# A third PSUM bank for the score gradients of two attention sweeps, taken from the sums and from a recurrent chain

## The chip, the cores and the metric

The kernel runs on one core of a Trainium2 chip. The metric is the device time of one execution in microseconds (us), the median of several. Runs of one kernel lie within 0.4% of each other; chips differ by about as much. So kernels are compared by ratios: a ratio is the mean time of a kernel's fast runs over the mean of the fast runs of the kernel before in the same rounds on the same chip, and thus not quite the ratio of the medians.

## The reference

Forward and backward of a gated mix of two attentions over 2048 tokens of width 576, in bf16. A has 32 query heads of size 18 and one shared key and value. B works on segments of 32 tokens, with eight memory rows that are the output of the segment before: 64 segments, one after the other.

```python
# A: shared-key attention (32 heads of 18)
scores = jnp.einsum('bhqd,bkd->bhqk', q, k) * Dh ** (-0.5)
p = _softmax(scores, axis=-1)
o = jnp.einsum('bhqk,bkd->bhqd', p, v)
# B: recurrent memory
for s in range(n_seg):
    h = jnp.concatenate([mem, xs], axis=1)
    ...
    o = jnp.einsum('bhte,hed->btd', o, Wo)
    mem = o[:, :M, :].copy()
# whole: g * a + (1 - g) * b, and the gradients of all weights, A_x and mem0
```

## The kernel before

A's attention is two sweeps of 1024 steps. A step makes scores S (128 x 1024), their exponential E on ScalarE, the gradient dP of the probabilities (two matmuls of 512 columns, one bank each of PSUM, where the kernel's matmuls leave their results), their products with E on VectorE, and adds E and the products into a sum (acc) on TensorE. B's recurrent chain is cut into 16 pieces a segment, and one piece is woven in front of each sweep step. Everything is issued in program order, and in the lines shown below TensorE starts its matmuls in that order. Shortened from the kernel:

```python
def weave(self, chain, sweep, per_piece):
    for _ in chain:                       # one piece of B's chain
        for _ in range(per_piece):        # per_piece = 1
            next(sweep, None)             # one step of A's sweep
# one step n of the backward sweep
mm_S(n + 1)                                               # b_S: one tile of 2 banks
dP = [psum.tile([P, 512], F32, name="b_dP", bufs=2) for _ in range(2)]
mm_u([t[:] for t in dP], n, 64)
ex(n + 1)                                                 # ScalarE: b_E = exp(b_S), 1024 columns
for i in range(2):                                        # VectorE: b_dS
    nc.vector.tensor_tensor(out=D_[n][:, i, :], in0=dP[i][:], in1=E_[n][:, i, :], op=ALU.mult)
# b_acc += products and E of step n - 1: 2 + 2 matmuls, column tiles of 32 (4 + 4 forward)
```

The 8 banks of 2 KiB are all in use. Forward: a_S 2, a_dP 2, a_acc 2, the chain's c_pj 1 and c_x 1. Backward: b_S 2, b_dP 2, b_acc 1, the chain's r_pj 2 and r_x 1. The chain needs two r_pj banks because it sums the new memory gradient in two column halves at once. Its backward pieces were: projection 3 and 2 of 5 row blocks, twice; dO transposed; score gradients; and then, with a `yield` (the end of a piece) after each,

```python
mem_grad(2, "r_pj", ...)   # 16 small matmuls
heads(2, 0)                # 32 matmuls of 288 columns into column half 0
mem_grad(0, "r_x", ...)
heads(2, 1)                # the same into column half 1
mem_grad(1, "r_x", ...)
heads(0, 0); heads(0, 1); heads(1, 0)      # a piece each
heads(1, 1); sums((0, 1))                  # one piece
sums((2, 3, 4))
```

## Time and profile before

| what | before |
|---|---|
| median of 3 runs | 6484.8 us (6476.7 to 6485.2) |
| forward sweep, first to last a_dP | 1928 us, 30.0 a segment of 16 steps |
| backward sweep, first to last b_dP | 1787 us, 27.3 a segment |
| all other stages together | 2756 us |
| TensorE, VectorE, ScalarE busy | 92%, 58%, 54% |

The two sweeps are 57% of the time, and only they are touched. A segment is read from the timeline as the distance between every sixteenth b_S (or a_S) matmul, a step as the distance between one and the next. The prediction below shows the lines.

### The profile page before, as it was taken

Reading aid. Unit: us, or ns where it says so; the run is one execution under the profiler, and the core shown is the slowest. Engines: PE = TensorE matmul, PEld = TensorE weight load, DVE = VectorE, ACT = ScalarE, POOL = GpSimd, SP = SyncE. Lnnn points to the kernel's source line nnn. Section 1 sums busy time; section 2 is a strip of 40 time slices with the busy share of each in tenths; the row PEclk is TensorE's granted clock in tenths of the full one; section 3 lists DMA queues with packets and bytes.
Section 4 is the critical chain, followed back from the end, with each engine's and each line's share of the span. In section 5 each row is a group of like instructions: output and inputs, shape, how many; then the busy total and the mean of one; then the engine's idle time right before and its main releaser. Section 6 shows DMA issues by size and latency. Waiting matters only on the chain. (4 is left out here: it accounts for less than half of the span.)

```text
span 6471.1 us, 208564 instructions
## 1 busy us (share of the span) xinstructions
PE 5931.5 (92%) x88611; PEld 3332.0 (51%) x88822; DVE 3769.7 (58%) x7061; ACT 3481.2 (54%) x5105; POOL 1952.8 (30%) x3451
## 2 busy tenths in 40 slices
PE   7898999999999995999879999999999899899997
PEld 5443444444444443778634444444444677675443
DVE  5336777777777773666568888888887211111111
ACT  3326777777777773656556767667776322211100
POOL 3002333333333333444423333333333111112212
PEclk9998999999999997999989999999999899999998
DMA  4636666666664435999854443333434799896643
GB/s 152 225 145 114 115 120 119 120 117 118 120 118 104 98 79 167 252 253 263 251 184 101 103 102 102 97 100 102 102 102 100 201 247 245 232 275 213 216 146 111
DMA packets 1368108, 991.94 MB, mean 153 GB/s; under 512 B 931613, under 2 KB 1184806, under 8 KB 1356486
## 3 DMA queue, kind: packets, MB, share of 16 engines
q1 hardware_dynamic: 1285030, 780.53, 49.3%
q0 software_dynamic: 82144, 198.05, 9.6%
q8 instruction: 696, 11.40, 0.7%
q14 instruction: 238, 1.95, 0.1%
HBM read 552.41 MB, written 384.76 MB: 145 GB/s over the span
## 5 line engine op out<-in xcount | busy, mean ns | idle before, releaser
L1424 DVE TENSOR_TENSOR a_W<-a_dP,a_E 128x512 bf16<-128x512 f32 x2048 | 1314.8, 684 | 478.9 <-PE a_dP L66 377.0
L1553 DVE TENSOR_TENSOR b_dS<-b_dP,b_E 128x512 bf16<-128x512 f32 x2048 | 1315.8, 684 | 328.0 <-PE b_dP L66 245.4
L1532 ACT ACTIVATE b_E<-b_S 128x1024 bf16<-128x1024 f32 x1024 | 1048.9, 1024 | 529.2 <-PE b_dP L66 393.6
L1394 ACT ACTIVATE a_E<-a_S 128x1024 bf16<-128x1024 f32 x1024 | 1052.1, 1027 | 134.5 <-PE a_dP L66 120.9
L66 PE MATMUL b_dP<-b_KV,b_QD 32*128 32x512 bf16 x2048 | 584.9, 382 | 5.2 <-DVE b_dS L1553 5.2
L66 PE MATMUL b_S<-b_KV,b_QD 32*128 32x512 bf16 x2048 | 401.6, 385 | 128.9 <-ACT b_E L1532 82.4
L66 PE MATMUL a_dP<-a_QD,l_KV 32*128 32x512 bf16 x2048 | 513.3, 382 | 1.0 <-DVE a_W L1424 0.8
L66 PE MATMUL w_acc<-w_d,w_h 128*128 128x512 bf16 (+1 forms) x2352 | 470.9, 379 | 2.5
L66 PE MATMUL a_S<-a_QD,l_KV 32*128 32x512 bf16 x2048 | 399.6, 383 | 74.3 <-ACT a_E L1394 72.4
L66 PE MATMUL r_pj<-WT,r_dT 128*32 128x288 bf16 x12288 | 447.0, 288 | 0.0
L66 PE MATMUL a_acc<-a_W,l_WK 128*32 128x512 bf16 x4096 | 410.5, 390 | 0.1
L66 PE MATMUL b_acc<-b_dS,b_SD 128*32 128x512 bf16 x2048 | 406.0, 393 | 0.0
L66 PE MATMUL b_acc<-b_E,b_SD 128*32 128x512 bf16 x2048 | 405.8, 393 | 0.0
L66 PE MATMUL a_acc<-a_E,l_VK 128*32 128x512 bf16 x4096 | 399.9, 380 | 0.0
L66 PEld LDWEIGHTS <-r_dT 128*32 128x32 bf16 x12288 | 330.6, 97 | 78.9 <-issue 1.1
L1027 DVE COPY y_T<-y_pt 128x512 bf16<-128x512 bf16 x256 | 96.8, 419 | 461.1 <-PE y_pt L71 443.6
L66 PEld LDWEIGHTS <-w_h 128*128 128x128 bf16 (+1 forms) x2400 | 213.1, 100 | 244.5 <-issue 3.4
L66 PEld LDWEIGHTS <-hm 128*32 128x32 bf16 x7680 | 207.0, 97 | 229.2 <-issue 15.0
L66 PEld LDWEIGHTS <-b_SD 128*32 128x32 bf16 x4096 | 105.3, 93 | 421.3 <-issue 420.3
L66 PEld LDWEIGHTS <-b_QD 32*128 32x128 bf16 x4096 | 142.9, 91 | 327.2 <-issue 245.3
L66 PEld LDWEIGHTS <-l_WK 128*32 128x32 bf16 x4096 | 105.3, 93 | 349.0 <-issue 348.9
L1013 ACT CAST y_tdk<-y_pk 128x512 bf16<-128x512 f32 x128 | 75.1, 587 | 379.9 <-PE y_pk L66 240.8
(410 smaller groups left out, 11558.8 us busy)
## 6 DMA issues: line engine op xcount, KB each, us to landing
b_QD<-qd_dram SPq DMA_DIRECT2D x256, 128.0 KB
b_SD<-sd_dram SPq DMA_DIRECT2D x256, 128.0 KB
dOx_dram<-p_tok SPq DMA_DIRECT2D x16, 1024.0 KB
c_vx<-vx_dram SPq DMA_DIRECT2D x256, 64.0 KB
krow_dram<-c_k POOLq DMA_DIRECT2D x64, 256.0 KB, 2.6
qrow_dram<-c_q POOLq DMA_DIRECT2D x64, 256.0 KB, 2.8
vrow_dram<-c_v POOLq DMA_DIRECT2D x64, 256.0 KB, 4.5
x_q<-qx_dram SPq DMA_DIRECT2D x32, 512.0 KB
```

Source lines behind the costliest of these rows:

```text
L66: return self.nc.tensor.matmul(out, lhsT, rhs, start=start, stop=stop, tile_position=tp, skip_group_check=True)
L1013: nc.scalar.copy(d[w][:, r, :], pk[:])
L1027: nc.vector.tensor_copy(T_[t][w][:], pt[:])
L1394: nc.scalar.activation(E_[n][:], S.pop(n)[:], ACT.Exp, scale=SCALEA)
L1424: nc.vector.tensor_tensor(out=W_[n][:, i, :], in0=dP[i][:], in1=E_[n][:, i, :], op=ALU.mult)
L1532: nc.scalar.activation(E_[n][:], S.pop(n)[:], ACT.Exp, scale=SCALEA)
L1553: nc.vector.tensor_tensor(out=D_[n][:, i, :], in0=dP[i][:], in1=E_[n][:, i, :], op=ALU.mult)
```

## The change

The intent: with three dP banks, the second dP matmul of a step no longer has to wait for the last product of the step before. Forward, the bank comes from the sums: one a_acc bank, so a new sum may start only when ScalarE has copied out the old one, and its first four matmuls are put off to the start of the next step. Backward, the bank comes from the chain: it finishes one column half before it begins the other, so one r_pj bank is enough, and its 48 head units (4 matmuls each) are dealt out anew.

```diff
 # backward chain
-            for j in range(2):
-                pj = psum.tile([P, 512], F32, name="r_pj", bufs=2)
-                for kts in ((0, 1, 2), (3, 4)):
+            pj = [psum.tile([P, 512], F32, name=nm, bufs=1) for nm in ("r_pj", "r_x")]
+            for k, parts in enumerate((((0, (0, 1, 2, 3)),), ((0, (4,)), (1, (0, 1))), ((1, (2, 3, 4)),))):
 ...
+            units = iter([(wi, hf, u) for hf in range(2) for wi in (2, 0, 1) for u in range(8)])
+            def heads(n):                       # n units of 4 matmuls
 ...
-            mem_grad(2, "r_pj", ...)
+            mem_grad(2, "r_x", ...)
 # pieces now: mem_grad 2 | mem_grad 0, 4 units | 4 units, mem_grad 1 | 6 | 6, x transposed | 4
 #             | 6 | 6, sums 0-1 | 6 | 6 | sums 2-4
 # forward sweep
+                if n > 1 and n % 16 == 1:
+                    acc = psum.tile([P, 512], F32, name="a_acc", bufs=1)
+                    acc_mm(acc, n - 1, E_, self.VK, True, False)
                 if n + 1 < NP_:
                     mm_S(n + 1)
-                dP = [psum.tile([P, 512], F32, name="a_dP", bufs=2) for _ in range(2)]
+                dP = [psum.tile([P, 512], F32, name="a_dP", bufs=3) for _ in range(2)]
 ...
-                if n % 16 == 0:
-                    acc = psum.tile([P, 512], F32, name="a_acc", bufs=2)
-                acc_mm(acc, n, E_, self.VK, n % 16 == 0, False)
+                if n == 0:
+                    acc = psum.tile([P, 512], F32, name="a_acc", bufs=1)
+                if n % 16 or n == 0:
+                    acc_mm(acc, n, E_, self.VK, n == 0, False)
 # backward sweep
-                dP = [psum.tile([P, 512], F32, name="b_dP", bufs=2) for _ in range(2)]
+                dP = [psum.tile([P, 512], F32, name="b_dP", bufs=3) for _ in range(2)]
```

More of the change, by code (lines that the diff above doesn't have):

```diff
@@ L846, in b_chain_bwd @@
             dOm = sp.tile([P, 8, E], BF16, name="r_dOm", bufs=1)
-            for j in range(2):
-                pj = psum.tile([P, 512], F32, name="r_pj", bufs=2)
-                for kts in ((0, 1, 2), (3, 4)):
-                    self.proj_part(pj, d_, self.WoT, j, kts)
-                    if s == NSEG - 1 and j == 0 and kts[0] == 3:
-                        self.load_WT()
-                    if kts[0] == 3:
-                        self.evac(dOm[:, 4 * j:4 * j + 4, :].rearrange("p u e -> p (u e)"), pj[:], use="s")
-                    yield
+            pj = [psum.tile([P, 512], F32, name=nm, bufs=1) for nm in ("r_pj", "r_x")]
+            for k, parts in enumerate((((0, (0, 1, 2, 3)),), ((0, (4,)), (1, (0, 1))), ((1, (2, 3, 4)),))):
+                for j, kts in parts:
+                    self.proj_part(pj[j], d_, self.WoT, j, kts)
+                    if kts[-1] == 4:
+                        self.evac(dOm[:, 4 * j:4 * j + 4, :].rearrange("p u e -> p (u e)"), pj[j][:], use="s")
+                if s == NSEG - 1 and k == 1:
+                    self.load_WT()
+                yield
             src = self.mem_T(dOm, psum, "r_x", 1)
@@ L886, in b_chain_bwd @@
             ph = {}
-            def heads(wi, hf):
-                if hf not in ph:
-                    ph[hf] = psum.tile([P, 288], F32, name="r_pj", bufs=2)
-                for u in range(8):
+            units = iter([(wi, hf, u) for hf in range(2) for wi in (2, 0, 1) for u in range(8)])
+            def heads(n):
+                for _ in range(n):
+                    wi, hf, u = next(units)
+                    if hf not in ph:
+                        ph[hf] = psum.tile([P, 288], F32, name="r_pj", bufs=1)
                     for g in range(4):
@@ L895, in heads @@
                                 start=(wi == 2 and u == 0), stop=(wi == 1 and u == 7), tp=(0, 32 * g))
-                if wi == 1:
-                    nc.scalar.copy(hs[:, 288 * hf:288 * hf + 288], ph[hf][:])
+                    if wi == 1 and u == 7:
+                        nc.scalar.copy(hs[:, 288 * hf:288 * hf + 288], ph[hf][:])
             def sums(kts):
@@ L904, in mem_grad @@
             def mem_grad(wi, name, pairs):
-                pg = psum.tile([P, 8, 32], F32, name=name, bufs=2 if name == "r_pj" else 1)
+                pg = psum.tile([P, 8, 32], F32, name=name, bufs=1)
                 for u in range(8):
@@ L912, in b_chain_bwd @@
             blk = lambda t, u0=0: [f(t[:, u0 + u]) for u in range(8)]
-            mem_grad(2, "r_pj", ((rows(mrow["dx"], E), [seln] * 8), (rows(dOm), blk(PqB))))
+            mem_grad(2, "r_x", ((rows(mrow["dx"], E), [seln] * 8), (rows(dOm), blk(PqB))))
             dSq = to_q((dS[:, 1, :],), "ds", nc.vector)
-            yield
-            heads(2, 0)
             yield
@@ L920, in b_chain_bwd @@
             self.expand(dSqB[:], dSq[:, 0, :, 0:8], 8)
+            heads(4)
             yield
-            heads(2, 1)
-            yield
+            heads(4)
             mem_grad(1, "r_x", ((rows(mrow["dx"]), [seln] * 8), (rows(mrow["q"]), blk(dSqB))))
@@ L928, in b_chain_bwd @@
             yield
-            heads(0, 0)
+            heads(6)
+            yield
+            heads(6)
             xq = to_q((pT[:, 0, :], dS[:, 0, :]), "x", nc.gpsimd)
@@ L934, in b_chain_bwd @@
             yield
-            heads(0, 1)
+            heads(4)
             yield
-            heads(1, 0)
+            heads(6)
             yield
-            heads(1, 1)
+            heads(6)
             pm = psum.tile([P, NKT, 8], F32, name="r_x", bufs=1)
             sums((0, 1))
+            yield
+            heads(6)
             if s:
                 PqB = p_blocks(nxt["pT"])
+            yield
+            heads(6)
             yield
```

## The prediction

> **What bounds the kernel now.** First the page: shares, then the costliest rows.
>
> ```profile
> PE 5931.5 (92%) x88611; PEld 3332.0 (51%) x88822; DVE 3769.7 (58%) x7061; ACT 3481.2 (54%) x5105; POOL 1952.8 (30%) x3451
> ...
> L1553 DVE TENSOR_TENSOR b_dS<-b_dP,b_E 128x512 bf16<-128x512 f32 x2048 | 1315.8, 684 | 328.0 <-PE b_dP L66 245.4
> L1532 ACT ACTIVATE b_E<-b_S 128x1024 bf16<-128x1024 f32 x1024 | 1048.9, 1024 | 529.2 <-PE b_dP L66 393.6
> ```
>
> No engine but TensorE is near full, and its 92% is modelled time. The change touches two sweeps: forward (a_dP matmuls, 508.5 to 2436.8 us by the view of that tile) and backward (b_dP, 3252.3 to 5039.6 us). Each is 1024 steps woven one to one with pieces of a recurrent chain, 16 to a segment. So I took the timeline of a segment and measured each step from its score matmul (b_S) to the next. A step with a light piece:
>
> ```profile
> 4019.85 0.39 PE L66 MATMUL b_S<-b_KV,b_QD 32*128 32x512 bf16 x2
> 4019.86 0.68 PE L66 MATMUL b_dP<-b_KV,b_QD 32*128 32x512 bf16 x2
> 4020.33 1.02 ACT L1532 ACTIVATE b_E<-b_S 128x1024 bf16<-128x1024 f32 x1
> 4020.38 1.29 DVE L1553 TENSOR_TENSOR b_dS<-b_dP,b_E 128x512 bf16<-128x512 f32 x2 [0.26 <-ACT r_dOm L63]
> 4020.47 0.39 PE L66 MATMUL b_acc<-b_dS,b_SD 128*32 128x512 bf16 x2
> ...
> 4020.70 0.82 PE L66 MATMUL r_pj<-WoT,dm 128*32 128x512 bf16 x12
> ...
> 4021.45 0.39 PE L66 MATMUL b_S<-b_KV,b_QD 32*128 32x512 bf16 x2
> ```
>
> Two things are to be seen. (1) The two b_dP matmuls span 0.68 us instead of 0.39: the second waits for the bank that VectorE's last multiply of the step before still reads (that multiply starts 0.53 us after b_S, lasts 1.29 and so reaches 0.27 us into a 1.55 us step). TensorE's queue stops behind it, and b_acc starts at 0.62. (2) ScalarE's loop has its own length: b_S to exponential 0.48, exponential 1.02, release to next b_S 0.05, together 1.55 us. The scores have one buffer, which the change leaves alone. Most light steps of the backward sweep take 1.55: no third bank shortens those.
>
> Heavy pieces show where the wait costs. Two steps with 32 r_pj matmuls each, the first with the wait, the second without:
>
> ```profile
> 4004.05 0.39 PE L66 MATMUL b_S<-b_KV,b_QD 32*128 32x512 bf16 x2 [0.23 <-ACT b_E L1532]
> ...
> 4004.06 0.68 PE L66 MATMUL b_dP<-b_KV,b_QD 32*128 32x512 bf16 x2
> ...
> 4004.67 0.39 PE L66 MATMUL b_acc<-b_dS,b_SD 128*32 128x512 bf16 x2
> ...
> 4004.90 1.15 PE L66 MATMUL r_pj<-WT,r_dT 128*32 128x288 bf16 x32
> 4005.98 0.10 PEld L66 LDWEIGHTS <-b_QD 32*128 32x128 bf16 x4 [0.24 <-issue]
> ```
>
> ```profile
> 4009.47 0.39 PE L66 MATMUL b_S<-b_KV,b_QD 32*128 32x512 bf16 x2
> 4009.48 0.39 PE L66 MATMUL b_dP<-b_KV,b_QD 32*128 32x512 bf16 x2
> ...
> 4009.80 0.39 PE L66 MATMUL b_acc<-b_dS,b_SD 128*32 128x512 bf16 x2
> ...
> 4010.02 1.15 PE L66 MATMUL r_pj<-WT,r_dT 128*32 128x288 bf16 x32
> ...
> 4011.11 0.39 PE L66 MATMUL b_S<-b_KV,b_QD 32*128 32x512 bf16 x2
> ```
>
> 1.93 against 1.64 us: b_acc at 0.62 against 0.33. From the second: b_S to chain piece 0.55, then 1.09 for 32 matmuls, 34 ns each. So a step is the longer of 1.55 (ScalarE's loop) and 0.55 + piece (TensorE), plus up to 0.30 of bank wait in the second case. One backward segment is
>
> ```profile
> 4000.56:4027.89 27.33, 25.83 (x499) 12.81 (x499) 22.64 (x41) 19.25 (x25) 9.16 (x17) 1.00 0.42 102
> ```
>
> 27.33 us (first figure after the window), of which VectorE is busy 22.64 (fourth); a forward segment, measured the same way from 1504.75 to 1534.77, is 30.0.
>
> **What the Trainium skill says.** "PSUM — Partial Sum Buffer", Specifications (TRN2): 8 banks of 2 KiB per partition, 512 fp32 values each. The code agrees: forward 2+2+2+1+1, backward 2+2+1+2+1 banks are all taken, so a third dP bank must be taken from somebody. "TensorE: Matmul & The Clock Gate", Part 3, The mechanism: matmuls start and end in strict order. The trace agrees: b_acc and the chain slide by 0.29 us with the waiting b_dP. The same part says that tiles in different row groups run together; b_S and b_dP start 10 ns apart. "Perfetto Trace Analysis", Optimization Strategy: consistent bubbles can mean that PSUM has no room for the next tile; the 0.3 us repeats in half of the steps.
>
> **The change, part by part.** No arithmetic is added or removed.
>
> (a) Third b_dP bank. The second dP of a step now needs the first multiply of the step before, which is done at 0.53 + 0.68 = 1.21 us, before the step ends. The wait goes. b_acc still needs the second multiply, but that ends at 0.27 to 0.28, before 0.33. So b_acc moves from 0.62 to 0.33 wherever it waited.
>
> (b) Backward chain regrouped to 4 or 6 units of 4 matmuls (16 or 24 instead of 32), which pays for r_pj's second bank. 24 matmuls are 24 x 0.034 = 0.82; 0.55 + 0.82 = 1.37, under 1.55. The 16 new pieces: weight-gradient-row piece 1.55; row gradient (0.50, first one at +0.10 for the change of tile shape) with 16 matmuls 0.33+0.33+0.45+0.54 = 1.65; the next, whose b_acc is held to 0.41 because VectorE first does the 0.17 + 0.45 us copy and transpose of dS, 0.41+0.23+0.54+0.10+0.50 = 1.78, call it 1.75; six, six and four units 1.55 each; the next six units behind the 0.70 us transpose of x (VectorE late by 0.4, b_acc near 0.74) 0.74+0.23+0.82 = 1.78; six units with two f32 sums (0.55) 1.90; six and six 1.55; the other sums behind a 0.43 us transpose 1.59; then projection and score pieces, 16 matmuls 0.55+0.97 = 1.52 and lighter ones, all at 1.55. Sum 24.8 + 0.10 + 0.20 + 0.23 + 0.35 + 0.04 = 25.72. Saved 27.33 - 25.72 = 1.61 per segment, 63 steady segments: 101 us. The first segment's 22.8 us stall (the timeline: b_QD loads queued behind the WT loads) stays.
>
> (c) Third a_dP bank. The heaviest wait:
>
> ```profile
> 1504.75 0.39 PE L66 MATMUL a_S<-a_QD,l_KV 32*128 32x512 bf16 x2 [0.16 <-ACT a_E L1394]
> 1504.76 0.73 PE L66 MATMUL a_dP<-a_QD,l_KV 32*128 32x512 bf16 x2
> ...
> 1505.42 0.40 PE L66 MATMUL a_acc<-a_W,l_WK 128*32 128x512 bf16 x4
> ...
> 1508.57 0.59 ACT L1429 COPY a_acs<-a_acc 128x512 f32<-128x512 f32 x1
> ```
>
> The forward chain is not regrouped: 20 matmuls of 512 columns are 1.19 us, so those steps stay bound by TensorE. By the timeline, a_acc starts at 0.67, 0.50, 0.50, 0.62 and 0.62 in the five TensorE-bound steps that wait (1504.75, 1510.68, 1516.44, 1521.80, 1527.28) and at 0.33 in steps that do not. Saved 0.30 + 0.17 + 0.17 + 0.30 + 0.30 = 1.24 per segment. The other waiting steps end on ScalarE's loop and gain nothing.
>
> (d) One a_acc bank. Once per segment the first new sum must wait for ScalarE's copy a_acs: 1508.57 + 0.59 = 1509.16, plus about 0.05, plus 0.22 for four matmuls, then a_S at 1509.43 instead of 1509.00: 0.43 lost. The step after regains 0.12, as its c_k copy no longer delays its exponential (0.48 instead of 0.60). Net +0.31.
>
> Forward 1.24 - 0.31 = 0.93 x 64 = 59 us. Total 101 + 59 = 160, so 6325 by the sum.
>
> **The rivals.** R1: the wait only moves from b_dP to b_acc, because both need VectorE. If it did in full, (c) gives 0, (d) costs 20, and the backward sweep keeps only what the shorter pieces give, some 30 us: about 6475. Against: 0.27 lies before 0.33; for: the margin is 0.05 us and VectorE has extra work in four pieces. R2: the single a_acc bank costs more, if a_acs falls behind a chain copy of 0.59 on ScalarE: 0.6 x 64 = 38 us more, 6363. R3: VectorE becomes the bound; 22.64 of 25.72 is 88%, so not on average, but each transpose may hold two steps instead of one: 0.5 x 64 = 32 us more. R4: everything backward sinks to 16 x 1.55 = 24.8, 58 us better than my sum: 6267; the f32 sums speak against it.
>
> **Range and chances.** The steps repeat to within 0.01 us from segment to segment, so the sums should be good; small waits that I did not see can only add. I shade 160 to 150: 6335 us, 8 in 10 between 6285 and 6395. Faster by over 2% means under 6355; most of my range is there: 0.77. Within 2%: 0.22. Slower: 0.01.
>
> **What would show it.** Right: both dP matmuls span 0.39 nearly everywhere; b_acc and a_acc at 0.33; backward segment near 25.7 with most steps at 1.55; forward near 29.1, with one step per segment where a_acc waits for a_acs; ScalarE's and VectorE's busy time unchanged. Wrong: b_acc still near 0.6 (R1), a forward segment near 30 (R2), VectorE pairs without gaps (R3), or longer waits at r_x, which now carries the second projection and all row gradients.

## The result, and the profile after

Median 6321.0 us of 4 runs (6318.0 to 6338.3), against 6485.0 before in the same rounds: ratio 0.9754, 95% interval 0.9733 to 0.9774. Repeated on another chip (the last experiment) it was 0.9741.

The page of the changed kernel, the same three rows as before:

```profile
PE 5710.0 (90%) x88822; PEld 3385.4 (54%) x88822; DVE 3755.0 (59%) x7061; ACT 3486.0 (55%) x5105; POOL 1956.0 (31%) x3451
...
L1564 DVE TENSOR_TENSOR b_dS<-b_dP,b_E 128x512 bf16<-128x512 f32 x2048 | 1313.2, 683 | 239.6 <-issue 119.9
L1543 ACT ACTIVATE b_E<-b_S 128x1024 bf16<-128x1024 f32 x1024 | 1048.9, 1024 | 444.3 <-PE b_dP L66 320.8
```

VectorE and ScalarE do the same work in the same busy time (1313 and 1049 us); only the idle time before them shrank. TensorE's busy time fell by 221 us though its work is the same, because matmuls that overlap are counted once: the two dP matmuls of a waiting step started up to 0.3 us apart before and start together now (b_dP busy 585 us before and 400 after, a_dP 513 and 399, with a mean of 382 to 386 ns for one matmul in all four; rows such as r_pj, 447 and 493 us, took some of it back).

A light step of the backward sweep after the change, from the timeline:

```profile
4136.37 0.39 PE L66 MATMUL b_S<-b_KV,b_QD 32*128 32x512 bf16 x2
4136.38 0.39 PE L66 MATMUL b_dP<-b_KV,b_QD 32*128 32x512 bf16 x2
...
4136.69 0.39 PE L66 MATMUL b_acc<-b_dS,b_SD 128*32 128x512 bf16 x2
...
4136.92 1.04 PE L66 MATMUL r_pj<-WoT,dm 128*32 128x512 bf16 x16
4137.92 0.39 PE L66 MATMUL b_S<-b_KV,b_QD 32*128 32x512 bf16 x2
```

The dP pair spans 0.39 us, b_acc starts at 0.32, and a piece of 16 projection matmuls (12 before) fits into 1.55 us. A forward and a backward segment of the changed kernel (stretch; length; busy time of TensorE, its weight loads, VectorE, ScalarE and GpSimd; clock, DMA share, GB/s):

```profile
1511.14:1540.43 29.29, 27.56 (x535) 13.74 (x536) 22.39 (x41) 22.48 (x31) 10.81 (x22) 1.00 0.70 119
4136.36:4161.93 25.57, 23.59 (x499) 13.28 (x499) 22.37 (x41) 19.21 (x24) 9.19 (x16) 1.00 0.41 109
```

29.3 us forward and 25.6 backward. The medians of each of the 16 steps over all segments say where it came from (row gradient 0 is `mem_grad(0)`, a unit is four matmuls of `heads`, the f32 sums are the matmuls of `sums`; steps in us; those not listed are unchanged within 0.03 in the forward sweep, and at the floor of 1.55 in the backward one):

| forward step | before | after |
|---|---|---|
| the five with a long piece that waited | 2.30, 2.12, 2.12, 2.25, 2.05 | 1.99, 1.95, 1.95, 1.95, 1.75 |
| with the start of a new sum | 1.95 | 2.48 |

| backward step (after the change) | predicted | measured |
|---|---|---|
| row gradient 0, 4 units | 1.65 | 1.76 |
| 4 units, row gradient 1 | 1.75 | 1.65 |
| 6 units behind the transpose of x | 1.78 | 1.61 |
| 6 units, two f32 sums | 1.90 | 1.93 |
| other sums | 1.59 | 1.55 |
| all others | 1.55 | 1.55 |

In the profiled runs the forward sweep is 43 us shorter and the backward one 122 us, together 165; the span is 152 us shorter. The missing 13 us lie in stages with the same code, and they are scatter: over thirteen profiles these stages took 2754 to 2770 us without pattern, 2756 in the one before, 2768 in this one and 2756 in the repeat of the changed kernel.

The one step that grew, in the forward sweep:

```profile
1513.13 0.39 PE L66 MATMUL a_S<-a_QD,l_KV 32*128 32x512 bf16 x2
...
1514.64 0.59 ACT L1439 COPY a_acs<-a_acc 128x512 f32<-128x512 f32 x1
...
1515.28 0.40 PE L66 MATMUL a_acc<-a_E,l_VK 128*32 128x512 bf16 x4
...
1515.61 0.39 PE L66 MATMUL a_S<-a_QD,l_KV 32*128 32x512 bf16 x2
```

The copy of the old sum ends at 1515.23, the first matmuls of the new one follow at 1515.28, and the scores behind them start 0.33 us later, 2.48 after the last.

### The profile page after: what moved, and what is told of

Read it like the earlier page. It is cut to its first block, busy times and chain, and to the rows that moved or that the text cites.

```text
span 6318.6 us, 209026 instructions
## 1 busy us (share of the span) xinstructions
PE 5710.0 (90%) x88822; PEld 3385.4 (54%) x88822; DVE 3755.0 (59%) x7061; ACT 3486.0 (55%) x5105; POOL 1956.0 (31%) x3451
## 4 chain that ended last, share of the span: by engine, by line
PE 64%; ACT 18%; issue 8%; DMA 6%; SPq 2%; POOL 1%; DVE 1%; ACTq 0%; POOLq 0%; DVEq 0%
ACT b_E L1543 10%; PE w_acc L66 10%; PE c_pj L66 7%; PE a_acc L66 6%; PE b_S L66 6%; ACT a_E L1401 5%; PE a_S L66 5%; PE p_pb L66 4%; PE r_pj L66 4%; DMA dsx_dram<-x_dS 3%; PE r_x L66 2%; PE x_tr L71 2%; PE b_acc L66 2%; PE c_x L66 2%; PE y_pdx L66 2%
## 5 line engine op out<-in xcount | busy, mean ns | idle before, releaser
L66 PE MATMUL r_pj<-WT,r_dT 128*32 128x288 bf16 x12288 | 493.3, 287 | 1.1 <-DMA WT<-st_WT 1.1
L66 PE MATMUL b_acc<-b_dS,b_SD 128*32 128x512 bf16 x2048 | 419.3, 390 | 0.4 <-DVE b_dS L1564 0.2
L66 PE MATMUL b_dP<-b_KV,b_QD 32*128 32x512 bf16 x2048 | 399.9, 386 | 0.0
L66 PE MATMUL a_dP<-a_QD,l_KV 32*128 32x512 bf16 x2048 | 398.7, 385 | 0.5 <-issue 0.5
L66 PEld LDWEIGHTS <-b_QD 32*128 32x128 bf16 x4096 | 164.5, 91 | 346.4 <-issue 284.9
L66 PEld LDWEIGHTS <-hm 128*32 128x32 bf16 x7680 | 222.1, 97 | 219.8 <-issue 37.0
L66 PEld LDWEIGHTS <-l_KV 32*128 32x128 bf16 x4096 | 135.1, 91 | 284.1 <-issue 259.7
L66 PE MATMUL y_pdx<-WT,y_T 128*128 128x288 bf16 x2048 | 273.3, 287 | 0.0
```

The source lines that it names most:

```text
L66: return self.nc.tensor.matmul(out, lhsT, rhs, start=start, stop=stop, tile_position=tp, skip_group_check=True)
```

## The experiments

My theory is the step rule of the prediction: the longer of ScalarE's loop (1.55 us) and TensorE's sequence (0.55 plus the piece), to which the wait for a dP bank adds up to 0.30. The rivals are those of the prediction: the wait only moves to acc (R1), the shared sum bank costs more than thought (R2), VectorE becomes the bound (R3). All outputs are right.

**1. The forward half alone.** The chain and the backward sweep are those of before.

```diff
 # backward chain and backward sweep as before the change
-                dP = [psum.tile([P, 512], F32, name="a_dP", bufs=2) for _ in range(2)]
+                dP = [psum.tile([P, 512], F32, name="a_dP", bufs=3) for _ in range(2)]
 # and one a_acc bank, as in the change
```

> Only the forward half of the change: three a_dP banks, one a_acc bank. My theory: the gains of the two sweeps are separate and add up. The trace of the changed kernel puts the forward sweep at 29.3 us a segment against 30.0, so 64 x 0.7 = 43 to 47 us less than before: about 6440 us, ratio 0.993. Rival (the single a_acc bank takes everything back, and all of the gain is backward): 6485, ratio 1.000. Rival (the wait for the bank was worth more forward, and something backward lost): under 6420.

Measured: 6446.4 us, ratio 0.9931 (0.9916 to 0.9946). Forward segment 29.3, backward 27.3. As expected.

**2. The backward half alone.**

```diff
 # forward sweep as before the change
-                dP = [psum.tile([P, 512], F32, name="b_dP", bufs=2) for _ in range(2)]
+                dP = [psum.tile([P, 512], F32, name="b_dP", bufs=3) for _ in range(2)]
 # and the backward chain of the change
```

> Only the backward half: three b_dP banks, and the chain regrouped so that it needs one r_pj bank. My theory: backward segment 25.6 us against 27.3, the sweep 122 us shorter in the profiled runs, so about 6363 us, ratio 0.981. Together with the forward-only kernel the two savings should give the full 158 to 164 us. Rival (they overlap or disturb each other through the DMA queues): the two savings miss the whole by over 25 us.

Measured: 6372.9 us, ratio 0.9816 (0.9801 to 0.9830). Segments 30.0 and 25.6. The two halves save 0.69% and 1.84%, 2.53% together; the whole saves 2.46% and 2.59% in its two measurements. Within the intervals they add up.

**3. The regrouped chain without its bank.**

```diff
-                dP = [psum.tile([P, 512], F32, name="b_dP", bufs=3) for _ in range(2)]
+                dP = [psum.tile([P, 512], F32, name="b_dP", bufs=2) for _ in range(2)]
```

> The changed kernel with b_dP back at two banks (one bank stays empty); the regrouped chain stays. My theory: bank and regrouping need each other. With the wait back, b_acc starts at 0.62 us again in steps after a short one, and a six-unit piece then makes 0.62+0.23+0.82 = 1.67 us, a 16-matmul projection 1.82; my sum over the 16 pieces is 27.0 to 27.4 us a segment, as before the change: 6321 + 63 x 1.6 = about 6420 us, ratio to before 0.990 (the forward gain alone). Rival (regrouping carries the backward gain, the bank is idle luck): 25.6 to 26.0 us a segment, about 6321 to 6345 us.

Measured: 6413.4 us, ratio 0.9887 (0.9871 to 0.9904), backward segment 26.95. The step with 16 projection matmuls, which took 1.55 above, is now

```profile
4191.12 0.39 PE L66 MATMUL b_S<-b_KV,b_QD 32*128 32x512 bf16 x2
4191.12 0.67 PE L66 MATMUL b_dP<-b_KV,b_QD 32*128 32x512 bf16 x2
...
4191.72 0.39 PE L66 MATMUL b_acc<-b_dS,b_SD 128*32 128x512 bf16 x2
...
4192.92 0.39 PE L66 MATMUL b_S<-b_KV,b_QD 32*128 32x512 bf16 x2
```

The dP pair spans 0.67 again, b_acc starts at 0.60 and the step takes 1.80: 1.82 was expected. So it is the bank that moves b_acc, which R1 denied. But the sum, 26.95, lies just under my 27.0 to 27.4: regrouping alone does bring 0.38 us a segment.

**4. The shared sum bank without the third dP bank.**

```diff
-                dP = [psum.tile([P, 512], F32, name="a_dP", bufs=3) for _ in range(2)]
+                dP = [psum.tile([P, 512], F32, name="a_dP", bufs=2) for _ in range(2)]
```

> The changed kernel with a_dP back at two banks (one bank stays empty); the single a_acc bank stays. It measures the price of the shared sums bank by itself. My theory: that price is 0.5 us a segment (the step with the wait for ScalarE's copy took 2.48 against 1.95 us) and is not hidden behind anything, so the forward segment is 30.4 to 30.5 us and the whole 6321 + 64 x 1.15 = about 6395 us, ratio 0.986. Rival (the copy's wait is hidden where the bank wait is there anyway): 30.0 us a segment, about 6366 us.

Measured: 6400.6 us, ratio 0.9861 (0.9846 to 0.9875), forward segment 30.57, so 0.55 over the 30.02 of before. The price of the shared bank is paid in full (a little over the 30.4 to 30.5 that I expected), and the third dP bank brings 30.57 - 29.28 = 1.29 us a segment against it.

**5. The third bank with the old large pieces.** The chain goes by column halves, but in six pieces of eight units, with the old four projection pieces.

```diff
-            heads(4) / heads(4) / heads(6) / heads(6) / heads(4) / heads(6) / heads(6) / heads(6) / heads(6)
+            heads(8) / heads(8) / heads(8) / heads(8) / heads(8) / heads(8)
+            # row gradients 0 and 1 in pieces of their own; projection (0, 1, 2), (3, 4) for each half
```

> The changed kernel with the third b_dP bank and the chain by column halves, but the heads in six pieces of eight units (32 matmuls) and the projection in the four old pieces: the bank without the regrouping. My theory: a piece of 32 matmuls takes 0.55 + 1.09 = 1.64 us with no wait for the bank; 10 light steps at 1.55, five heavy ones at 1.64, one at 2.2 with the f32 sums and 0.4 to 0.5 more behind the transpose of x: 26.4 us a segment, so the bank alone brings 0.9 of the 1.7 us and the regrouping the rest: 6321 + 63 x 0.8 = about 6371 us, ratio 0.982. Rival (bank and regrouping only work together, as the kernel with two b_dP banks suggests): 27 us or more, 6410 us.

Measured: 6347.8 us, ratio 0.9811 (0.9795 to 0.9828), backward segment 26.10; most steps with 32 head matmuls take 1.64 to 1.68. So of the 1.76 us backward the bank alone (with the order by halves) brings 27.33 - 26.10 = 1.23, where I expected 0.9, regrouping alone (with the same order) 0.38, both 1.76: the parts sum to 1.61, so most of it is a plain sum. The rival, that they only work together, falls, and so does my reading in experiment 3 that they need each other. What the order by halves does by itself, with two banks and the old pieces, no run tests.

**6. The first matmuls of a new sum behind dP.** They do not change, only their place in TensorE's order.

```diff
-                if n > 1 and n % 16 == 1:
-                    acc = psum.tile([P, 512], F32, name="a_acc", bufs=1)
-                    acc_mm(acc, n - 1, E_, self.VK, True, False)
                 if n + 1 < NP_:
                     mm_S(n + 1)
 ...             # the two dP matmuls
+                if n > 1 and n % 16 == 1:
+                    acc = psum.tile([P, 512], F32, name="a_acc", bufs=1)
+                    acc_mm(acc, n - 1, E_, self.VK, True, False)
```

> The changed kernel with the first matmuls of a new forward sum moved from ahead of the next scores to behind the next dP matmuls, so that TensorE does not stand before the scores while ScalarE copies the old sum. My theory: the cost of the single a_acc bank is the place of the wait, not the copy: the two steps concerned take 1.93 + 1.87 = 3.80 us instead of 2.48 + 1.65 = 4.13, so 0.33 x 64 = 21 us less than the changed kernel: about 6300 us, ratio to before 0.971. Rival (the copy is on ScalarE's own loop, and moving the matmuls only moves the wait): no change, 6321.

Measured: 6296.4 us, ratio 0.9726 (0.9711 to 0.9740), forward segment 28.99 instead of 29.28. The two steps take 1.94 + 1.90 = 3.84 instead of 4.13 us:

```profile
1508.27 0.59 ACT L1439 COPY a_acs<-a_acc 128x512 f32<-128x512 f32 x1
1508.70 0.39 PE L66 MATMUL a_S<-a_QD,l_KV 32*128 32x512 bf16 x2
...
1509.03 0.40 PE L66 MATMUL a_acc<-a_E,l_VK 128*32 128x512 bf16 x4
```

The scores now start while the copy still runs (it ends at 1508.86), and the new sum's matmuls find it done. The wait cost so much by its place in TensorE's order. By the ratio alone the gain over the changed kernel (0.9754 and 0.9741) is not clear of noise; it is read from the steps. What is left of the price, 3.84 against 1.95 + 1.68 = 3.63 before the change, is about the 0.22 us of the four matmuls that moved: the step that they left gets no shorter, for the chain's next piece waits there for ScalarE's copy c_k (it ends at 1507.46, the piece starts at 1507.51).

**7. The transpose of x earlier.**

```diff
             self.expand(dSqB[:], dSq[:, 0, :, 0:8], 8)
+            for i, t in enumerate((pT[:, 0, :], dS[:, 0, :])):
+                nc.gpsimd.tensor_copy(pads["x"][:, i, :, 0:8], u8(t))
 ...
             heads(6)
+            nc.vector.transpose(xq[...], pads["x"][...])     # and its stores
             yield
             heads(6)
-            xq = to_q((pT[:, 0, :], dS[:, 0, :]), "x", nc.gpsimd)
```

> The changed kernel with GpSimd's copies for the 0.70 us transpose of x two pieces earlier and the transpose one piece earlier, so that the step which then starts b_acc late is the one with only four units. My theory: the 1.98 us step of the backward segment is late because VectorE stood before that transpose; it falls to 1.55 and the segment from 25.6 to 25.2: 0.43 x 63 = 27 us less, about 6294 us, ratio to before 0.970. Rival (any 0.7 us on VectorE costs the same wherever it is put, VectorE being near its limit): 6321.

Measured: 6301.1 us, ratio 0.9734 (0.9720 to 0.9749), backward segment 25.51 instead of 25.57. A miss. I had taken the step of 1.98 us from one segment of the trace; the median of that step over all segments is 1.61, and it did fall to 1.55. There were 0.06 us to win, not 0.43.

**8. The scores in two halves.** The same two banks, as two tiles, each with its own exponential.

```diff
-            S[n] = psum.tile([P, 2, 512], F32, name="b_S", bufs=1)
+            S[n] = [psum.tile([P, 512], F32, name="b_S", bufs=2) for _ in range(2)]
 ...
-            nc.scalar.activation(E_[n][:], S.pop(n)[:], ACT.Exp, scale=SCALEA)
+            for i, t in enumerate(S.pop(n)):
+                nc.scalar.activation(E_[n][:, i, :], t[:], ACT.Exp, scale=SCALEA)
 # the same for a_S
```

> The changed kernel with the scores in two tiles of one bank each and two exponentials of 512 columns in place of one of 1024, in both sweeps: the same two banks. It tests the floor of 1.55 us. My theory: that floor is ScalarE's loop (exponential 1.02, release 0.05, scores 0.48); with halves the loop is about 1.1 us, TensorE (0.55 + piece) and VectorE (1.22 a pair plus chain work, about 1.43 on average) bind instead, and the light steps fall well below 1.55: backward segment 23 to 24 us, forward 27.5 to 28.5, together 150 to 250 us less: 6070 to 6170 us, ratio to before 0.935 to 0.952. Rival (the floor is VectorE's: two multiplies and what it adds for the chain): light steps stay at 1.5 us, 6290 us or more.

Measured: 6303.6 us, ratio 0.9737 (0.9723 to 0.9752), segments 29.48 forward (0.2 longer) and 25.27 backward (0.3 shorter). The largest miss. The floor itself is what I said: single steps fall to 1.15 us. But they only borrow:

```profile
4109.74 0.39 PE L66 MATMUL b_S<-b_KV,b_QD 32*128 32x512 bf16 x2
...
4110.16 1.08 ACT L1545 ACTIVATE b_E<-b_S 128x512 bf16<-128x512 f32 x2 [0.69 <-PE b_dP L66]
...
4110.89 0.78 PE L66 MATMUL b_S<-b_KV,b_QD 32*128 32x512 bf16 x2
...
4111.30 0.39 PE L66 MATMUL b_dP<-b_KV,b_QD 32*128 32x512 bf16 x2
...
4113.06 0.39 PE L66 MATMUL b_S<-b_KV,b_QD 32*128 32x512 bf16 x2
```

The next b_S pair starts after 1.15 us, but spans 0.78: its second half waits for the second exponential, which ends 0.42 + 1.08 = 1.50 us after the first b_S, and TensorE's queue with dP, acc and the piece stands behind it. That step takes 2.17. The two are 3.32 us together, against 1.55 + 1.76 = 3.31 for the same steps of the changed kernel. A loop was shortened, but the wait for the second half was left in the middle of TensorE's order. The forward steps borrow in the same way (1.55 and 1.95 became 1.16 and 2.44). The Trainium skill's page "Perfetto Trace Analysis", Optimizing Scalar/DVE Operations, says that breaking up instructions may let work finish sooner where an unsaturated engine causes bubbles on another. Here the first half did finish sooner; that it brought almost nothing I put down to the order of the matmuls, by these lines. An order that avoids it was not tried, so this is not shown.

**9. A kernel with all that was learned.** Experiments 6 and 7, and the head units dealt out by what else lies in the piece.

```diff
-            heads: 4, 4, 6, 6, 4, 6, 6, 6, 6 units
+            heads: 3, 3, 7, 7, 4, 7, 3, 7, 7 units
 # with the edits of experiments 6 and 7
```

> The changed kernel with three further moves: the first matmuls of a new forward sum behind the dP matmuls (as measured alone: 0.29 us a forward segment), the transpose of x one piece earlier, and the head units of the backward chain dealt out by what else lies in the piece: 3, 3, 7, 7, 4, 7, 3, 7, 7 instead of 4, 4, 6, 6, 4, 6, 6, 6, 6. My theory: a backward step is the longer of 1.55 and 0.55 + piece, a unit is 0.136 us, so the three steps over the floor fall from 1.76, 1.65 and 1.93 to 1.63, 1.55 and 1.55 while seven units (0.55 + 0.95 = 1.50) stay under it: 25.57 to 24.9 us a segment, 42 us less, and 18 us forward: ratio to before 0.966. Rival (the units that leave one step lengthen the others as much, TensorE being the bound throughout): 0.972, the forward part alone.

Measured: 6251.3 us, ratio 0.9655 (0.9639 to 0.9671), segments 28.99 and 24.99. The step with the two f32 sums, 1.93 in the changed kernel:

```profile
4055.76 0.39 PE L66 MATMUL b_S<-b_KV,b_QD 32*128 32x512 bf16 x2
...
4056.31 0.54 PE L66 MATMUL r_pj<-WT,r_dT 128*32 128x288 bf16 x12
4056.78 0.61 PE L66 MATMUL r_x<-selF,r_hs 128*128 128x8 f32 x4
4057.33 0.39 PE L66 MATMUL b_S<-b_KV,b_QD 32*128 32x512 bf16 x2
```

It takes 1.57. The steps of seven units stay at 1.55. This kernel beats both the kernel before and the changed one (0.9741 on the same chip, with intervals that do not meet). Its backward segment came out near the 24.9 that the two-term rule gave; the step with three units and row gradient 1 stays at 1.61, where I expected 1.55. The forward gain is that of experiment 6.

**10. More work for VectorE.**

```diff
                     nc.vector.tensor_tensor(out=D_[n][:, i, :], in0=dP[i][:], in1=E_[n][:, i, :], op=ALU.mult)
+                scr = sp.tile([P, P], F32, name="b_scr", bufs=1)
+                nc.vector.tensor_copy(scr[:], self.zeros[:])
```

> The changed kernel with one more VectorE instruction in each backward step, a 128x128 copy of zeros to an unused tile, behind the two multiplies. It asks if VectorE is a bound after the change. My theory: VectorE is idle 0.25 us before each pair of multiplies in a light step, so a copy of 0.15 to 0.2 us is hidden there, and only steps behind chain work on VectorE grow: 0 to 0.5 us a segment, 0 to 30 us in all. Rival (VectorE is the bound): the copy is paid in full, 1024 x 0.15 to 0.2 = 150 to 200 us more.

Measured: 6330.0 us, ratio 0.9770 (0.9753 to 0.9788), against 0.9741 (0.9726 to 0.9755) for the changed kernel on the same chip. The row of the added copy (minimum, median and maximum duration in ns):

```profile
L1566 DVE CAST b_scr<-zeros x1024: 204/217/1443, 3216.6 to 4896.7; 128x128 f32<-128x128 bf16 x171
```

At the median these sum to 222 us, but they overlap with their neighbours: VectorE's busy time rose by 126 us, from 3755 to 3881. The backward segment grew from 25.57 to 25.83 us, which is 17 us in all, in two steps that lie behind chain work on VectorE; the other fourteen did not move by 0.01. So VectorE is not the bound (R3), though it has little room in those two steps.

**11. The changed kernel again,** without an edit.

> The changed kernel unaltered, for comparison with the other two on this chip. Every theory: ratio to before 0.975 within 0.002.

Measured: 6309.9 us, ratio 0.9741 (0.9726 to 0.9755), segments 29.28 and 25.57, as in the first profile to 0.01.

## Why the prediction was right or wrong

The time (6335 predicted, its plain sum 6325, measured 6321) and the mechanism were right. That the plain sum is right to 4 us is partly luck: its forward part was too large by 12 to 16 us and its backward part too small by 10 to 21 (see Total).

- **The bank wait goes (a).** Right: b_acc's median start, 0.43 to 0.62 in the eleven steps where it was late (0.62 in seven), is now 0.32 to 0.33 in all 16, and a_acc's, 0.49 to 0.67 in eight steps, likewise. R1 falls by the trace after, and experiment 3 brings the late b_acc back with the two banks.
- **ScalarE's loop as the floor.** Right as to 1.55 us: 12 of the 16 backward steps have their median there after the change, and experiment 8 breaks it in single steps. What the prediction did not need to say, and what I then expected wrongly, is what lies right behind the floor.
- **Backward pieces (b).** 25.72 predicted, 25.57 measured, by terms that err both ways. The step with row gradient 0 took 0.11 more: I gave its 16 small matmuls 0.45 us and the change to the units nothing, and the trace has 0.49 from the first small matmul to the first unit and 0.61 from there to the next scores for 0.54 of matmuls. The step after it took 0.10 less, because a longer step before it left no hold on its b_acc. The step behind the transpose of x took 0.17 less: in the segment from 4136.36 VectorE starts its multiplies before the transpose has ended (at 4152.98, against 4152.36 + 0.70), 0.79 us after b_S instead of 0.53, so late by 0.26 and not by 0.4.
- **Forward bank (c).** 1.24 us a segment predicted; the five steps gained 0.31 + 0.17 + 0.17 + 0.30 + 0.30 = 1.25, and experiment 4 against the changed kernel gives 1.29.
- **One a_acc bank (d).** This term was mis-sized: +0.31 predicted, +0.50 measured (0.53 in one step, 0.03 back in the next). Two parts. I let the scores follow the sum's four matmuls after 0.22 us; they follow after 0.33, where TensorE changes from column tiles to row tiles. The Trainium skill's page "TensorEngine Tiling (Array Packing)", Key Properties, says that a change of the tiling mode drains TensorE; the page gives no time, and this trace shows about 0.1 us more (see the last section). And I had the next step regain 0.12 as if it stood on ScalarE's loop; it is bound by TensorE at 1.65. R2 was thus right that the bank costs more than my sum, by 0.19 us a segment and not 0.6, but not in its reason: the copy a_acs stands behind no chain copy (it starts at 1514.64, as the exponential before it ends). Experiment 6 removes over half of the cost.
- **Total.** Forward, 64 x (30.02 - 29.28) = 47 us where 59 were predicted, and 43 in the profile. Backward, 63 x (27.33 - 25.57) = 111 where 101 were predicted, and 122 in the profile. The other 11 us are mostly irregular steps: what the steps of the sweep exceed their medians by is 15 us before and in experiment 1, with the old chain, and 5 to 6 in the changed kernel, its repeat and experiment 2, with the new one (the first segment apart). About 5 us of this is three spells of half clock, each 6.8 us long and 1.8 us dear (three in experiment 1 too, none in the changed kernel, one short one in its repeat and in experiment 2). The rest is mostly one step in every thirteenth segment, longer by 1.1 to 1.5 us before and by 0.37 after. What causes either no run tests.

R3 is refuted by experiment 10, and R4 (all steps at the floor) by the four steps above it; experiment 9 comes within 0.2 us a segment of it. The last sign that the prediction named, longer waits at r_x, did not come in any size: TensorE's idle time before matmuls into r_x was 41 us before and is 48 after.

## What to carry to other kernels

Write the time of a step as the longest of a few loops (each engine's own loop with its buffer, and the in-order queue of the busiest engine), and ask of a buffer which loop it shortens: this bank paid only in steps where TensorE's queue was the longest, and nothing where ScalarE's was. Where pieces of a second task are woven in, deal them out so that no step exceeds the floor that the other loop sets anyway. Where an in-order engine must wait, put the waiting instruction behind work that others wait for; and judge a step by its median over all repetitions, not by one reading of the timeline.

## What the Trainium skill lacked or had wrong

- "TensorEngine Tiling (Array Packing)", Key Properties: a change of the tiling mode drains TensorE, without a time. Here, after the first of four 512-column matmuls in column tiles, further column tiles start 0.23 us later (4136.69 to 4136.92), row tiles 0.33 (1515.28 to 1515.61) and full 128x128 tiles 0.33 (4144.45 to 4144.78): about 0.1 us a change.
- "Perfetto Trace Analysis", Identifying the Most-Contended Engine: matmul busy time is no good measure of the distance to roofline. A further reason that the page does not give: two matmuls in different row groups are counted once where they run together and nearly twice where one is held up (b_dP busy 585 us before and 400 after, with the same 2048 matmuls of 382 and 386 ns).
- "Perfetto Trace Analysis", Optimizing Scalar/DVE Operations: breaking up instructions. It lacks the warning that the wait for the second half may then hold up all that stands behind it on the other engine: one step fell from 1.55 to 1.15 us and the next rose from 1.76 to 2.17.
